# Loading the last rows of wo on all 16 DMA engines, and one wo block ahead of the last V tile, in a four-layer decode attention kernel

## Chip, cores and metric

The kernel runs on one core of a Trainium2 chip. The metric is the device time of one execution in microseconds (us). Every comparison of times is made between runs of the same rounds on the same chip. The single positions in time come from one profiled execution of each kernel, and these are compared across rounds and chips. The granted clock is the share of TensorE's full clock that the profile shows as let through.

## The reference

Two attention blocks, A and B, are applied in the order A, B, A, B to one token `x` of 640 elements. Each block has 32 heads of 192 and caches of 8192 keys and values per head, all in bf16.

```python
def block(x, k_cache, v_cache, wq, wo):            # x: 1 x 1 x 640
    q = (x @ wq).reshape(1, 1, 32, 192).transpose(0, 2, 1, 3)
    scores = einsum("bhqd,bhkd->bhqk", q, k_cache) * 192 ** -0.5
    o = einsum("bhqk,bhkd->bhqd", softmax(scores), v_cache)
    return o.transpose(0, 2, 1, 3).reshape(1, 1, 32 * 192) @ wo
for w in (A, B, A, B):
    x = x + block(layernorm(x), w.k_cache, w.v_cache, w.wq, w.wo)
```

One K or V tile (one head) is 3 MiB. Layers 2 and 3 use the caches of layers 0 and 1 again; the kernel keeps K and V of head 0 of layer 0, and V of heads 28 to 31 of layer 1, on chip for that.

## The kernel before

All large transfers go through one pool of eight slots, each as large as a K or V tile. A list `plan` gives the order of the transfers, a list `steps` the order of the computation, and a transfer is issued as soon as the step that frees its slot is done.

```python
O_LAST = 2; HEADS_W = 10; NSLOT = 8; AHEAD = 4
KEPT = {0: {("k", 0), ("v", 0)}, 1: {("v", 28), ("v", 29), ("v", 30), ("v", 31)}}
...
    O_PART = [P // 2, P // 2, P // 2, P]      # partitions of the last wo rows, by layer
    OI = [O_LAST * DH // n for n in O_PART]   # rows of wo on one partition: 6, 6, 6, 3
```

The output projection of a layer is made in three blocks of ten heads ("wo") and the last two heads ("wol", 384 rows of wo, 480 KB). In layers 0 to 2 the wol rows lie on 64 partitions and are loaded by two transfers of 32 partitions:

```python
            if n[0] == "wol":
                r0 = o["wol"] * DH
                if O_PART[l] == P:
                    return SP.op(lambda s: s.dma_start(
                        wol_rows(l), w["wo"][r0:r0 + O_LAST * DH].rearrange("(p i) n -> p (i n)", p=P)), ...)
                k = O_PART[l] // O_LAST
                for h in range(O_LAST):
                    e = SP.op(lambda s, h=h: s.dma_start(
                        wol_rows(l)[h * k:(h + 1) * k],
                        w["wo"][r0 + h * DH:r0 + (h + 1) * DH].rearrange("(q e i) n -> e q (i n)", e=8, i=OI[l])), ...)
```

The end of a layer in the two lists (m: q times K and the sums S; s: softmax; v: values; wc: transposes ten heads' outputs into oT):

```python
                    if p == H - 1:
                        part.append(("s", l, p))
                        part += [("v", l, i) for i in range(H - AHEAD, H)]
                        part.insert(-O_LAST, ("wc", l, 2))
                steps += part
                plan += [n for n in part if n[0] == "v" and first_load(*n) == n]
            ...
            plan.append(("wo", l, 2));  steps.append(("wo", l, 2))
            plan.append(("wol", l));    steps.append(("wol", l))
```

After a head's values, its outputs are reshaped for the projection one step later. The function that does it is held in `todo`:

```python
                elif n[0] == "v":
                    if todo is not None:
                        todo()
                    values(n[2])
                    todo = (lambda h=n[2]: gather(h)) if n[2] < H - O_LAST else (lambda h=n[2]: gather_last(h))
                ...
                elif n[0] == "wo":
                    if todo is not None:
                        todo()
                        todo = None
                    ...
                    last["oT"] = project(n, slot[place[n]][:, 0:k * D], oT[:, 0:k], last["oTw"])
                else:                                    # wol
                    last["TT"] = last["TTn"]
                    last["oTl"] = ev_y = project(n, wol_rows(l), oTl[0:O_PART[l]], last["TTn"])
```

`wol` does not call `todo`: the `wo` step just ahead of it has.

Of the kernel before, what the change touches and what calls it, by code (L numbers as in the profile page):

```python
# [71 lines left out]
def build(nc, A_x, A_k, A_v, A_wq, A_wo, B_x, B_k, B_v, B_wq, B_wo, out):  # L72
    _, H, SK, DH = A_k.shape
    D = A_x.shape[-1]
    P = 128
# [3 lines left out]
    NL = 4  # L79
# [5 lines left out]
    TS = J * DH  # L85
    QW = H * DH
    Q_PARTS = [[(0, 2), (2, 2), (4, 1)] if l < 2 else [(0, 1), (1, 2), (3, 2)] for l in range(NL)]
    O_PART = [P // 2, P // 2, P // 2, P]
    OI = [O_LAST * DH // n for n in O_PART]
    NB = 3  # L90
    G = 4
# [3 lines left out]
                    wo=[H - HEADS_W, O_LAST, O_LAST + HEADS_W], wol=0)  # L95
    ORDER = [FORWARD, FORWARD, FORWARD, BACKWARD]

    with ExitStack() as ctx:
# [84 lines left out]
        def head(l, p):  # L183
            return ORDER[l]["heads"][p]

        def first_load(kind, l, p):

            n = (kind, head(l, p))
            if l >= 2 and n in KEPT[l - 2]:
                return (kind, l - 2, ORDER[l - 2]["heads"].index(n[1]))  # L190
            return (kind, l, p)

        def stays(kind, l, p):
            return l < 2 and (kind, head(l, p)) in KEPT[l]

        steps, plan = [], []
        for l in range(NL):
            if l < 2:
                plan.append(("wq", l, 0))
                steps += [("wq", l, g) for g in range(3)]  # L200
            elif l == 2:
                plan += [("wq", l, g) for g in range(3)]
                steps.append(("wq", l, 0))
            else:
                plan.append(("wq", l, 0))
                steps.append(("wq", l, 0))
            for p in range(H):
                if p in (HEADS_W, 2 * HEADS_W):
                    b = p // HEADS_W - 1
                    steps += [("wc", l, b), ("wo", l, b)]  # L210
                    plan.append(("wo", l, b))
                if first_load("k", l, p) == ("k", l, p):
                    plan.append(("k", l, p))
                if stays("k", l, p):
                    plan.append(("t", l, p))
                if l == 2 and p == 0:
                    part = [("m", l, 0), ("wq", l, 1), ("s", l, 0), ("v", l, 0), ("wq", l, 2)]
                elif p < H - AHEAD:
                    part = [("m", l, p), ("s", l, p), ("v", l, p)]
                else:  # L220
                    part = [("m", l, p)]
                    if p > H - AHEAD:
                        part.append(("s", l, p - 1))
                    if p == H - 1:
                        part.append(("s", l, p))
                        part += [("v", l, i) for i in range(H - AHEAD, H)]
                        part.insert(-O_LAST, ("wc", l, 2))
                steps += part
                plan += [n for n in part if n[0] == "v" and first_load(*n) == n]
                if l == 3 and p == 1:  # L230
                    for g in (1, 2):
                        plan.append(("wq", l, g))
                        steps.append(("wq", l, g))
            plan.append(("wo", l, 2))
            steps.append(("wo", l, 2))
            plan.append(("wol", l))
            steps.append(("wol", l))
        plan.append(("wob", NL - 1))
# [46 lines left out]
        def wol_rows(l):  # L285
# [3 lines left out]
            else:  # L289
                i = place[("wq", l + 1, 0)] * TS + (DC * QW if l == 0 else QC)  # L290
            return pool[0:O_PART[l], i:i + OI[l] * D]

        def transfer(n):
# [4 lines left out]
# [4 lines that stand above are left out]
                        wol_rows(l), w["wo"][r0:r0 + O_LAST * DH].rearrange("(p i) n -> p (i n)", p=P)),  # L302
                        *free, sem=semOL, inc=16)
                k = O_PART[l] // O_LAST
                for h in range(O_LAST):
# [74 lines left out]
        def layer(l, ev_z, ev_true):  # L380
# [155 lines left out]
            def values(h):  # L536
# [18 lines left out]
                else:  # L555
                    q = 1 if O_PART[l] == P else O_PART[l] // O_LAST // 8
                    parts = [(o_sb[:, i * DH:(i + 1) * DH].rearrange("p (i e q) -> p q e i", i=OI[l], q=q),
# [19 lines left out]
            def gather_last(h):  # L577

                n = O_PART[l] // O_LAST
                k = OI[l]  # L580
# [73 lines left out]
def bass_interleave_layers__gqa_block_cached__mha_block_cached__decode_kernel(  # L654
    nc: bass.Bass,
    A_x: bass.AP,
    A_k_cache: bass.AP,
    A_v_cache: bass.AP,
    A_wq: bass.AP,
    A_wo: bass.AP,  # L660
    B_x: bass.AP,
    B_k_cache: bass.AP,
    B_v_cache: bass.AP,
    B_wq: bass.AP,
    B_wo: bass.AP,
    out: bass.AP,
):
    build(nc, A_x, A_k_cache, A_v_cache, A_wq, A_wo, B_x, B_k_cache, B_v_cache, B_wq, B_wo, out)
# [28 lines left out]
```

## Time and profile before

| | before |
|---|---|
| time, median of the first 3 runs | 1998.22 us (1997.81 to 1998.73) |
| span of the profiled run | 1996.3 us |
| moved by DMA | 849.69 MB, mean 426 GB/s |

The page of the kernel before: its first line, the GB/s line of the 40 slices (each 49.9 us), the DMA sum, and the chain of waits by engine.

```profile
span 1996.3 us, 20649 instructions
...
GB/s 412 429 432 428 431 430 429 431 430 430 429 431 429 430 430 430 429 430 430 429 379 430 430 431 428 432 429 430 431 429 426 431 428 431 430 430 430 429 430 335
DMA packets 40296, 849.69 MB, mean 426 GB/s; under 512 B 4688, under 2 KB 4688, under 8 KB 5136
...
DMA 69%; PE 18%; DVE 11%; ACT 1%; issue 1%; another core or an unknown queue 0%; SPq 0%; DVEq 0%
```

The kernel waits for DMA, which runs at 430 GB/s in nearly all slices. The exceptions are the first, the last, and slice 21 with 379: the change from layer 1 to layer 2. The same place in windows of 10 us (last column GB/s; before it the DMA share and the granted clock):

```profile
1010.00:1020.00 10.00, 6.75 (x171) 5.66 (x163) 0.00 (x0) 2.23 (x6) 0.00 (x0) 0.95 0.72 301
1020.00:1030.00 10.00, 7.83 (x100) 4.29 (x93) 5.57 (x13) 0.73 (x2) 0.54 (x1) 0.50 0.88 345
1030.00:1040.00 10.00, 9.14 (x136) 3.40 (x121) 3.80 (x6) 0.44 (x2) 0.00 (x0) 0.84 1.03 403
```

The timeline of the issuing queue at that place (start, duration, what is issued):

```profile
986.37 0.33 SPq L333 DMA_DIRECT2D pool<-in_B_wo_dram  x1
996.10 1.43 SPq L306 DMA_DIRECT2D pool<-in_B_wo_dram  x2
997.58 0.44 SPq L327 DMA_DIRECT2D pool<-in_A_wq_dram  x1
1020.50 6.25 SPq L327 DMA_DIRECT2D pool<-in_A_wq_dram  x2
1035.35 0.34 SPq L322 DMA_DIRECT2D pool<-in_A_k_cache_dram  x1
```

Layer 2's wq is loaded in three pieces. The second has to wait for the slot of the final wo block (issued at 1020.50), the third for the first piece's, and the next K (head 1) for the slot of the kept K of head 0, whose last use is layer 2's first product (issued at 1035.35). The timeline of TensorE there (the text in brackets says how long the engine was idle before, and what ended it):

```profile
1009.43 1.47 PE L546 MATMUL O<-pool,p_sb 128*2 128x384 bf16 x32
...
1017.31 3.16 PE L465 MATMUL YB<-oT,pool 128*128 128x1 bf16 x75 [1.13 <-DMA pool<-in_B_wo_dram]
1020.40 1.35 PE L465 MATMUL YB<-oTl,pool 64*128 64x1 bf16 x30
...
1023.39 1.78 PE L407 MATMUL QM<-wq,xb 128*128 128x384 bf16 x5 [0.52 <-DVE xb L386]
1024.96 1.39 PE L427 MATMUL QT<-xb,pool 128*128 128x1 bf16 x45
1027.48 0.61 PE L508 MATMUL S<-pool,ident 128*128 128x512 bf16 x1 [1.13 <-DVE pool L495]
1027.88 7.44 PE L58 MATMUL S<-pool,ident 128*128 128x512 bf16 x23
```

The first line is the values of head 30. So there is a tail: the last block lands (1017.26), 75 and 30 matmuls for the projection, the layer norm, the first q, the product with K, the 23 sums, and only then the next K.

The page counts 16 DMA engines, and the trace records 16 landings of each of these transfers (V31: 16 from 1002.72 to 1011.52); each is taken here as the landing of one engine's share. Worked out from these records (us; the spread is from the fastest engine to the slowest):

```
transfer that lands at         fastest   slowest   spread
  496 (V, layer 0)              492.55    496.26     3.7
  530 (wq of layer 1)           523.87    529.56     5.7
 1011 (V31, layer 1)           1002.72   1011.52     8.8
 1029 to 1031 (wq of layer 2)  1029.34   1031.46     2.1
 1506 (V, layer 2)             1501.60   1505.99     4.4
 1517 (wq of layer 3)          1510.78   1517.30     6.5
 1984 (V, layer 3)             1974.16   1983.87     9.7
```

In these rows the engines drift apart (3.7 us at 496, 8.8 at 1011) and come together only after the queue has run dry (131 GB/s from 1018 to 1020; 2.1 at 1029). The kernel goes on at the slowest: the final wo block's last landing is at 1017.26, and the 75 matmuls that wait for it start at 1017.31.

### The profile page before, as it was taken

Reading aid. Unit: us, or ns where it says so; the run is one execution under the profiler, and the core shown is the slowest. Engines: PE = TensorE matmul, PEld = TensorE weight load, DVE = VectorE, ACT = ScalarE, POOL = GpSimd, SP = SyncE. Lnnn points to the kernel's source line nnn. Section 1 sums busy time; section 2 is a strip of 40 time slices with the busy share of each in tenths; the row PEclk is TensorE's granted clock in tenths of the full one; section 3 lists DMA queues with packets and bytes.
Section 4 is the critical chain, followed back from the end, with each engine's and each line's share of the span. In section 5 each row is a group of like instructions: output and inputs, shape, how many; then the busy total and the mean of one; then the engine's idle time right before and its main releaser. Section 6 shows DMA issues by size and latency. Waiting matters only on the chain.

```text
span 1996.3 us, 20649 instructions
## 1 busy us (share of the span) xinstructions
PE 1397.3 (70%) x10555; PEld 321.0 (16%) x7611; DVE 1047.7 (52%) x1074; ACT 220.3 (11%) x665; POOL 4.5 (0%) x22
## 2 busy tenths in 40 slices
PE   4667767667576766666777676776776768767776
PEld 1111112111311211211041111121112212111112
DVE  3554554556255456455725545545663455654563
ACT  0111111111011111111011111111101111111111
POOL 0000000000000000000000000000000000000000
PEclk9888877889678788888977878888887788887888
DMA  9999999999999999999999999999999999999997
GB/s 412 429 432 428 431 430 429 431 430 430 429 431 429 430 430 430 429 430 430 429 379 430 430 431 428 432 429 430 431 429 426 431 428 431 430 430 430 429 430 335
DMA packets 40296, 849.69 MB, mean 426 GB/s; under 512 B 4688, under 2 KB 4688, under 8 KB 5136
## 3 DMA queue, kind: packets, MB, share of 16 engines
q1 hardware_dynamic: 40064, 848.38, 99.3%
q8 instruction: 71, 1.16, 0.2%
q14 instruction: 17, 0.14, 0.0%
q10 hardware_dynamic: 144, 0.00, 0.0%
HBM read 848.36 MB, written 0.00 MB: 425 GB/s over the span
## 4 chain that ended last, share of the span: by engine, by line
DMA 69%; PE 18%; DVE 11%; ACT 1%; issue 1%; another core or an unknown queue 0%; SPq 0%; DVEq 0%
DMA pool<-in_B_k_cache_dram 32%; DMA pool<-in_A_k_cache_dram 30%; PE S L58 12%; DVE pool L495 9%; DMA pool<-in_B_wo_dram 4%; PE O L546 2%; DMA pool<-in_A_wo_dram 2%; DMA x_bf<-in_A_x_dram 1%; PE S L508 1%; PE TB L569 1%; PE QT L427 1%; DVE s_sb L516 1%; PE YB L465 1%; ACT p_sb L526 1%; PE TB L530 0%
## 5 line engine op out<-in xcount | busy, mean ns | idle before, releaser
L495 DVE TENSOR_TENSOR pool<-pool,q_sb 128x3072 bf16<-128x3072 bf16 x512 | 865.7, 1754 | 398.8 <-DMA pool<-in_A_k_cache_dram 204.7
L58 PE MATMUL S<-pool,ident 128*128 128x512 bf16 x2944 | 803.4, 427 | 34.6 <-DVE pool L495 34.5
L546 PE MATMUL O<-pool,p_sb 128*2 128x384 bf16 x4096 | 340.1, 414 | 0.0
L508 PE MATMUL S<-pool,ident 128*128 128x512 bf16 x128 | 61.3, 479 | 223.9 <-DVE pool L495 223.9
L516 DVE TENSOR_REDUCE s_sb<-S 128x64 f32<-128x512 f32 x128 | 88.4, 690 | 237.0 <-PE S L58 237.0
L569 PE MATMUL TB<-o_sb,small 128*1 128x192 f32 x480 | 123.9, 391 | 38.1 <-DVE small L534 27.1
L546 PEld LDWEIGHTS O<-pool,p_sb 128*2 128x2 bf16 x4096 | 128.1, 87 | 128.1 <-issue 91.8
L453 ACT ACTIVATE q_sb<-QM 128x192 bf16<-128x192 f32 x120 | 39.6, 330 | 964.1 <-PE QM L446 964.1
L446 PEld LDWEIGHTS QM<-ident,qT 128*128 128x128 bf16 x240 | 23.2, 98 | 745.3 <-issue 729.8
L530 PE MATMUL TB<-small,ones 128*128 128x1 f32 x256 | 50.3, 266 | 109.9 <-ACT p_sb L526 109.9
L520 PE MATMUL QM<-ident,m_bf 128*128 128x128 bf16 x128 | 27.8, 217 | 122.9 <-DVE m_bf L519 121.2
L561 ACT ACTIVATE o_sb<-O,small 128x384 f32<-128x384 f32 (+1 forms) x136 | 77.2, 579 | 224.5 <-PE O L546 224.5
L534 DVE RECIPROCAL small<-TB 128x1 f32<-128x1 f32 x128 | 21.6, 168 | 122.9 <-PE TB L530 122.9
L526 ACT ACTIVATE p_sb<-s_sb,small 128x64 bf16<-128x64 f32 x128 | 44.5, 348 | 268.5 <-DVE small L523 268.5
L523 DVE TENSOR_REDUCE small<-QM 128x1 f32<-128x128 f32 x128 | 37.3, 292 | 63.3 <-PE QM L520 63.3
L575 ACT ACTIVATE orow<-TB 1x192 bf16<-1x192 f32 x120 | 38.3, 319 | 202.7 <-PE TB L569 202.7
L530 PEld LDWEIGHTS TB<-small,ones 128*128 128x128 f32 x256 | 39.5, 194 | 130.4 <-ACT p_sb L526 130.4
L508 PEld LDWEIGHTS S<-pool,ident 128*128 128x128 bf16 x128 | 12.8, 100 | 283.6 <-DVE pool L495 283.3
L520 PEld LDWEIGHTS QM<-ident,m_bf 128*128 128x128 bf16 x128 | 12.3, 96 | 216.7 <-ACT q_sb L453 126.9
L569 PEld LDWEIGHTS TB<-o_sb,small 128*1 128x1 f32 x480 | 33.5, 89 | 81.4 <-DVE small L534 36.0
L465 PE MATMUL YB<-oT,pool 128*128 128x1 bf16 x900 | 38.1, 178 | 6.6 <-DMA pool<-in_A_wo_dram 3.2
L465 PEld LDWEIGHTS YB<-oT,pool 128*128 128x128 bf16 x900 | 37.0, 131 | 7.6 <-DMA pool<-in_A_wo_dram 3.4
(50 smaller groups left out, 220.0 us busy)
## 6 DMA issues: line engine op xcount, KB each, us to landing
pool<-in_B_k_cache_dram SPq DMA_DIRECT2D x64, 3072.0 KB, 35.5
pool<-in_A_k_cache_dram SPq DMA_DIRECT2D x63, 3072.0 KB, 27.7
pool<-in_A_v_cache_dram SPq DMA_DIRECT2D x63, 3072.0 KB, 33.5
pool<-in_B_v_cache_dram SPq DMA_DIRECT2D x60, 3072.0 KB, 37.0
pool<-in_A_wo_dram SPq DMA_DIRECT2D x6, 2400.0 KB, 25.8
pool<-in_B_wo_dram SPq DMA_DIRECT2D x5, 2400.0 KB, 33.9
pool<-in_A_wq_dram SPq DMA_DIRECT2D x1, 7680.0 KB, 20.9
pool<-in_B_wq_dram SPq DMA_DIRECT2D x1, 7680.0 KB, 29.5
```

Of the source, the lines that this page charges most:

```text
L58: return t.add_instruction(mybir.InstMatmult(name=t.bass.get_next_instruction_name(), engine=mybir.EngineType.PE, ins=[t.lower_ap(rhs), t. ...
L453: lambda a: a.activation(q_sb[i][:], QM[:, 0:DH], ACT.Copy), e, last["q"][i], bank=use["QM"])
L465: e = PE.op(lambda t, i=i, c=c, f=y_first[0], fin=end and i == k - 1: t.matmul(YB[:, c:c + 1], lhsT=t3[:, i, c:D:DC], rhs=o[:, i:i + 1], s ...
L495: e = DV.op(lambda v, d0=d0: v.tensor_tensor(k3[:, :, d0:d0 + QD], kin[:, :, d0:d0 + QD], q_sb[qi][:, d0:d0 + QD].unsqueeze(1).broadcast_t ...
L508: t.matmul(S[:, :], lhsT=ident[:], rhs=k3[:, :, d0:d0 + R], start=True, stop=fin) if d0 == 0 else
L516: ev_s = DV.op(lambda v: v.tensor_reduce(s_sb[par][:], S[:].rearrange("p (j r) -> p j r", r=R), AX.X, ALU.add), ev_S[h], last["s"][par], b ...
L520: e = PE.op(lambda t: t.matmul(QM[:, C_MX:C_MX + P], lhsT=m_bf[par][:, 0:1].broadcast_to([P, P]), rhs=ident[:], start=True, stop=True), ev ...
L526: ev_p[h] = AC.op(lambda a: a.activation(p_sb[pi][:], s_sb[par][:], ACT.Exp, bias=negm[par][:, 0:1], accum_out=l_col[par][:]), ev_n, ev_s, ...
L530: e = PE.op(lambda t: t.matmul(TB[:, C_L + par:C_L + par + 1], lhsT=ones[:, 0:1].broadcast_to([P, P]), rhs=l_col[par][:], start=True, stop ...
L546: e = PE.op(lambda e, g=g, j=j, f=m < G, fin=fin: e.matmul(OB[par][32 * g:32 * g + 2, 0:2 * DH], lhsT=p_sb[pi][:, j:j + 2], rhs=t[:, j * D ...
L561: ev_os[h] = AC.op(lambda a, o=o, i=i: a.activation(o, i, ACT.Copy, scale=rl[pi][:, 0:1]), e, ev_rl[h], last["osb"], bank=use[f"O{par}"])
L569: e = PE.op(lambda t, i=i: t.matmul(TB[0:1, C_O:C_O + DH], lhsT=pick[:, i:i + 1], rhs=o_sb[:, i * DH:(i + 1) * DH], start=(i == 0), stop=( ...
```

## The change

The intent: load the wol rows on all 128 partitions and so on all 16 engines in every layer (in before's trace the two transfers of such a layer have 16 landings together, two on each of eight engines by their order and spacing, and two more records, one 1.1 to 1.2 us after each issue); and, in layer 1 alone, load the final wo block ahead of V of head 31, so that its projection is over and its slot free while V31 is still in flight.

```diff
-    O_PART = [P // 2, P // 2, P // 2, P]
+    O_PART = [P] * NL
...
                         part.insert(-O_LAST, ("wc", l, 2))
+                        part.insert(-1 if l == 1 else len(part), ("wo", l, 2))
                 steps += part
-                plan += [n for n in part if n[0] == "v" and first_load(*n) == n]
+                plan += [n for n in part if n[0] == "wo" or n[0] == "v" and first_load(*n) == n]
...
-            plan.append(("wo", l, 2))
-            steps.append(("wo", l, 2))
             plan.append(("wol", l))
             steps.append(("wol", l))
```

With the new order in layer 1 the `wo` step comes before V31, so nothing calls `todo` after V31: head 31's outputs never reach oTl there, and the projection takes the rows that layer 0 left. The output check cannot see it: every run was correct by it.

## The prediction

> **What bounds the kernel now.** DMA. The page gives 849.69 MB at 426 GB/s over 1996.3 us; the chain of waits is 69% DMA. Steady slices run at about 430 GB/s. Two stand out: number 21 (layer 1 to 2, 379 GB/s) and the last (335). 10 us windows from 1010 to 1040 moved 301, 345 and 403 GB/s: about 5.6 us lost at 430 GB/s.
>
> **Why there.** Four V tiles of layer 1 stay in the eight slots, so little can be queued. The timeline: the final wo block lands at 1017.26; its 75 matmuls take 3.16 us, 30 for the last rows 1.35 us; at 1020.50 the second piece of the next wq is issued, and only when layer 2's head 0 has been multiplied and summed (1035.35) the next K[...].
>
> **The last wo rows.** The landing times in the trace show the 16 engines drifting apart: slowest minus fastest is 8.8 us by 1011, is reset by the dry queue at 1023 to 1037, and is 9.7 us at the end. Each load of the last rows (480 KB) adds 2.3 us to eight engines and nothing to the others[...]. After: 16 engines, 1.15 us each (estimate: half of 2.3). But slow engines are in both groups: at 1011 the eight stand at up to 8.8 us, the others at up to 8.0; at the end 9.7 and about 8.1. Evening out moves the maximum by -0.4 to +0.4 us, not by 1.15 per layer.
>
> **The reordering.** wo lands one V transfer (7.3 us) earlier, near 1010; its 75 matmuls run near 1012.4 to 1015.6, while V31 is in flight. The second wq piece is issued about 5 us earlier, before the slow engines run dry. V31 lands where wo did (about 1017.5). After it come 32 value matmuls (1.47 us) and 15 for the last rows (0.7 us) instead of 4.5 us.
>
> **What was dropped.** The changed kernel's instruction order lacks, in layer 1 alone, head 31's reshaping into oTl (L585 and L590, 2.2 us from the values' end to the copy's). The projection there takes layer 0's rows for that head. I expect this to pass: one head adds some 5e-6 to values of 0.05 in bf16 (estimate). With it, the tail after V31 would be about 4.4 us and the reordering would gain nothing at the next K.
>
> **Sum.** Layer 2's xb, the third wq piece and the next K come about 2 us earlier; from there the queue is full to the end, so this carries through. Evening out adds 0.4 us in the second half. Predicted 1995.8 us (before 1998.2), 8 in 10 between 1993.0 and 1997.8. Faster by over 2%: 0.01; within 2%: 0.98; slower: 0.01.
>
> **What would show it.** Windows 1010 to 1040: about 2 us less lost; the wq issue near 1015.6, the next K's near 1033.4; landing spread no longer growing by 2 us at the last wo rows; slices 11 and 31 (the other layer changes) unchanged.
>
> **What would make it wrong.** If the slow engines are mostly among the eight, each layer gives 1.15 us and the gain is 4 to 5 us. If the drift falls otherwise (single packets cost one engine 1.6 us), 1 to 2 us either way.

1998.2 less 2 us at the next K less 0.4 us from evening out is the forecast of 1995.8. What before's trace shows:

- The last rows of each of layers 0 to 2 have 16 landings in two transfers, two on each of eight engines. The second comes 2.3 us after the same engine's landing of the wo block ahead (505.57 to 507.90, 1010.62 to 1012.94, 1507.31 to 1509.65). That the others get nothing shows in the first wq piece of layer 2: it lands 3.48 us after that block on one of them (1008.43 to 1011.91), 5.78 us after it on one of the eight (1010.62 to 1016.40).
- The next K's first packets start 1.0 us after its issue (1036.34 for 1035.35).
- The 1.6 us: in 263 pairs of large transfers that follow each other, at least 15 engines keep their distances to 0.25 us, and in 60 of these pairs one engine falls 1.45 to 1.63 us (median 1.54) behind the other 15. In each of the 60, exactly one packet of 16384 bytes of the queue that the page calls "q8 instruction" (71 in the span, mean 1.07 us) lies between that engine's two landings; of stretches as long (8.85 us) laid along the span, 27% hold one.

## The result

| | before | after |
|---|---|---|
| median | 1998.01 us (1996.92 to 1998.73, 4 runs) | 1996.08 us (1995.43 to 1997.06, 4 runs) |
| span of the profiled run | 1996.3 us | 1994.7 us |

The ratio is 0.9991, with a 95% interval of 0.9974 to 1.0009. (A ratio is the mean time of one kernel's fast runs over that of the other's of the same rounds, so it is not quite the ratio of the medians.) The interval includes 1: no gain in time is shown by these runs. The forecast was 1995.8 us. The output check cannot see the missing head 31: every run was correct by it.

Line numbers from L228 on are lower by one in the changed kernel. Its page:

```profile
span 1994.7 us, 20387 instructions
...
GB/s 411 431 431 428 431 428 430 430 432 429 429 429 431 428 432 429 429 431 428 430 384 431 430 429 432 428 430 429 430 430 426 429 431 429 431 429 430 430 429 344
DMA packets 40487, 849.67 MB, mean 426 GB/s; under 512 B 4688, under 2 KB 4688, under 8 KB 5328
...
DMA 69%; PE 17%; DVE 12%; ACT 1%; issue 1%; another core or an unknown queue 0%; DVEq 0%
```

Its windows at the layer change:

```profile
1010.00:1020.00 10.00, 6.04 (x117) 4.46 (x115) 0.00 (x0) 0.17 (x1) 0.00 (x0) 0.58 0.97 394
1020.00:1030.00 10.00, 7.82 (x79) 3.34 (x68) 6.31 (x14) 1.68 (x4) 0.54 (x1) 0.50 0.82 329
1030.00:1040.00 10.00, 9.14 (x142) 3.49 (x125) 3.06 (x6) 0.44 (x2) 0.00 (x0) 0.84 0.88 346
```

The gap of 1010 to 1020 is gone (394 for 301), but the next two windows lost what it gained (329 for 345, 346 for 403): in sum 1069 for 1049, which is 0.5 us of transfer at 430 GB/s. The issuing queue shows why:

```profile
976.05 0.33 SPq L332 DMA_DIRECT2D pool<-in_B_wo_dram  x1
986.40 0.33 SPq L321 DMA_DIRECT2D pool<-in_B_v_cache_dram  x1
996.13 0.33 SPq L300 DMA_DIRECT2D pool<-in_B_wo_dram  x1
...
1013.65 12.36 SPq L326 DMA_DIRECT2D pool<-in_A_wq_dram  x2
1034.77 0.34 SPq L321 DMA_DIRECT2D pool<-in_A_k_cache_dram  x1
```

The second wq piece goes out 6.85 us earlier, the next K only 0.58 us. TensorE between the two:

```profile
1010.47 3.16 PE L464 MATMUL YB<-oT,pool 128*128 128x1 bf16 x75
1017.58 2.73 PE L545 MATMUL O<-pool,p_sb 128*2 128x384 bf16 x32 [3.96 <-DMA pool<-in_B_v_cache_dram]
1020.24 0.77 PE L464 MATMUL YB<-oTl,pool 128*128 128x1 bf16 x15
...
1022.65 1.78 PE L406 MATMUL QM<-wq,xb 128*128 128x384 bf16 x5 [0.53 <-DVE xb L385]
1024.22 1.39 PE L426 MATMUL QT<-xb,pool 128*128 128x1 bf16 x45
1026.74 0.61 PE L507 MATMUL S<-pool,ident 128*128 128x512 bf16 x1 [1.13 <-DVE pool L494]
1027.14 7.60 PE L58 MATMUL S<-pool,ident 128*128 128x512 bf16 x23
```

V31 landed at 1017.53, where the wo block had landed before. But its 32 value matmuls took 2.73 us, not 1.47 as the forecast had taken from before (its line at 1009.43): the granted clock was 0.50 from 1011.65 to 1032.13.

From the landing records, the load of the last rows no longer widens the spread by 2 us in layer 2: 3.7 us at 1510 and 3.6 us at 1515 (before: 4.4 and 6.5). The packet records of the layer 0 to 1 change give 64 packets of 7680 bytes at a mean of 294 ns before, and 128 of 3840 bytes at 154 ns after: 8 on each of eight engines are 2.4 us, 8 on each of 16 engines 1.2 us (by the landings, two transfers of eight engines each and one of 16).

### The profile page after: what moved, and what is told of

Read it like the earlier page. It is cut to its first block, busy times and chain, and to the rows that moved or that the text cites. A ratio compares the mean times of both kernels' runs of the same rounds, so it can differ in the third digit from the quotient of the medians.

```text
span 1994.7 us, 20387 instructions
## 1 busy us (share of the span) xinstructions
PE 1392.3 (70%) x10426; PEld 317.9 (16%) x7482; DVE 1047.4 (53%) x1074; ACT 220.2 (11%) x664; POOL 4.5 (0%) x22
## 3 DMA queue, kind: packets, MB, share of 16 engines
q8 instruction: 70, 1.15, 0.2%
## 4 chain that ended last, share of the span: by engine, by line
DMA 69%; PE 17%; DVE 12%; ACT 1%; issue 1%; another core or an unknown queue 0%; DVEq 0%
DMA pool<-in_B_k_cache_dram 32%; DMA pool<-in_A_k_cache_dram 30%; PE S L58 11%; DVE pool L494 10%; DMA pool<-in_B_wo_dram 2%; PE O L545 2%; DMA pool<-in_A_wo_dram 2%; DMA pool<-in_B_v_cache_dram 2%; DMA x_bf<-in_A_x_dram 1%; PE S L507 1%; PE TB L568 1%; PE QT L426 1%; DVE s_sb L515 1%; ACT p_sb L525 1%; PE YB L464 1%
## 5 line engine op out<-in xcount | busy, mean ns | idle before, releaser
L545 PE MATMUL O<-pool,p_sb 128*2 128x384 bf16 x4096 | 346.9, 420 | 4.0 <-DMA pool<-in_B_v_cache_dram 4.0
```

The source lines that it names most:

```text
L545: e = PE.op(lambda e, g=g, j=j, f=m < G, fin=fin: e.matmul(OB[par][32 * g:32 * g + 2, 0:2 * DH], lhsT=p_sb[pi][:, j:j + 2], rhs=t[:, j * D ...
```

## How the time is split in the experiments

Four terms make up the span of each profiled run: when the last block that layer 1's tail starts from (wo before, V31 in the new order) has landed; from there to the start of the 23 S matmuls of layer 2's head 0 (the tail); those matmuls, to the issue of the next K; and the rest, to the end. In us, worked out from each kernel's trace:

```
run            landed   tail   S    next K    rest    span
before        1017.26  10.62  7.47  1035.35  961.00  1996.35
after         1017.53   9.61  7.63  1034.77  959.96  1994.73
after_again   1017.39   9.59  6.59  1033.57  960.23  1993.80
even_only     1017.34   9.97  6.53  1033.84  960.43  1994.27
even_again    1017.48   9.93  7.40  1034.81  961.18  1995.99
even_drop31   1017.72   9.92  6.74  1034.38  960.67  1995.05
even_l2       1016.96  10.62  7.06  1034.64  960.47  1995.12
even_l01      1017.88   9.92  7.83  1035.63  960.69  1996.32
order_only    1016.93  10.19  7.89  1035.01  961.61  1996.62
gather_back   1017.40  11.62  7.80  1036.82  959.98  1996.80
warm          1017.77   8.99  6.66  1033.42  960.45  1993.87
late          1017.82  17.88  6.67  1042.37  959.92  2002.29
```

The tail repeats to 0.05 us between kernels with the same instructions in it; the S term and the rest vary by up to 1.4 us from run to run. That is why the tail can be read from a single trace, while 5 rounds of times leave an interval of about 0.25%, or 5 us. The traced run was the fastest of its five in after_again, even_only, even_l2, even_drop31, gather_back and warm (warm: 1995.67 us, its other four 1997.63 to 1998.68), so S and rest of one trace don't stand for the kernel. The S matmuls take 6.5 to 7.9 us. In all twelve traces they take the longer, the later after their start the clock comes back: 2.8 us after it in even_only (6.53), 5.5 in order_only (7.89). It came back at 1029.87 in after_again (6.59) and at 1030.07 in even_only (6.53), at 1032.13 in after (7.63) and 1034.36 in gather_back (7.80).

## The experiments

My theory after the result: the even load gains little through the engines' drift and 0.65 us through 15 instead of 30 matmuls; the order gains what the shorter tail after V31 leaves; the time follows the issue of the next K. Rivals: the even load gains its 1.15 us in each layer, or the early second wq piece is the gain. The first four kernels ran on one chip, the next three on another, the last four together again; each group has nine runs of the kernel before.

### after_again: the changed kernel once more

> The changed kernel once more, as the yardstick of this group. Both theories: 1995.5 to 1996.8 us, 1.3 to 2.3 us under before. The next K of layer 2 (its head 1) is issued within 1 us of 1034.8, its slowest landing about 0.3 us ahead of before's; the landing spread stays near 3.4 us over the first load of the last wo rows.

Measured: 1996.06 us against 1998.88 for before in this group, ratio 0.9988 (0.9975 to 1.0000). The gain of 2.8 us is over the expected 1.3 to 2.3. The next K went out at 1033.57, 1.2 us earlier than in the first trace, where 1 was allowed; 1.0 us of that are the S matmuls, which ran at full clock from 1029.87 on. The tail is the same as in the first trace. The second wq piece went out at 1016.83 here, 3.2 us later than in the first trace, and yet the next K earlier: the early piece is not what sets it. The windows from 1010 to 1040 moved 1119 in sum, 1.6 us of transfer more than before's 1049, where the first trace had 0.5. The spread did not stay near 3.4 us over the first load: it went from 3.75 (last V of layer 0) to 4.77 (wq of layer 1); in before it went from 3.71 to 5.69.

### even_only: the load on 16 engines alone

```diff
-    O_PART = [P // 2, P // 2, P // 2, P]
+    O_PART = [P] * NL
```

> Only the 16-engine load of the last wo rows, with the old order and all of head 31. Theory (slow engines sit in both groups of eight, so evening moves the slowest one little; the gain at the layer 1 to 2 change comes from the order): 0.2 to 1.2 us under before, the final wo block of layer 1 landing within 0.5 us of before's 1017.3, the next K issued within 0.7 us of 1035.35. Rival (the eight are the slow ones, each layer gives its 1.15 us): 2.3 to 3.4 us under before, as much as or more than the whole change.

Measured: 1997.28 us against 1998.88, ratio 0.9991 (0.9979 to 1.0004): 1.6 us by the medians, between the two theories' ranges. The positions in the trace decide: wo landed at 1017.34, not 1.15 us earlier, so the rival fails for the first half. The tail is 0.65 us shorter. The next K went out 1.5 us earlier, more than the 0.7 allowed, 0.9 us of it in the S matmuls. This kernel is complete: head 31 is in it. Its projection, where the last rows take 0.74 us for before's 1.35:

```profile
1017.43 3.16 PE L465 MATMUL YB<-oT,pool 128*128 128x1 bf16 x75
1020.45 0.74 PE L465 MATMUL YB<-oTl,pool 128*128 128x1 bf16 x15
```

### order_only: the new order alone, rows still on eight engines

The changed kernel with `O_PART = [P // 2, P // 2, P // 2, P]`.

> Only the new order (with the missing head 31 of layer 1), the last rows still on eight engines. Theory: V31 lands at about 1017.3, the second wq piece is issued before 1015, but the values and the last rows run at a granted clock of 0.5, so the next K is issued only 0 to 1 us before 1035.35; 0 to 1 us under before. Rival (the order alone is the change's gain): 1.5 to 2.3 us under before.

Measured: 1998.36 us against 1998.88, ratio 0.9994 (0.9980 to 1.0008). The next K at 1035.01 and the small gain are as the theory has them; the second wq piece, expected before 1015, went out at 1016.38. The tail is 0.43 us shorter. The values took 2.73 us here too.

### gather_back: the changed kernel with head 31's reshaping put back

```diff
                 else:
+                    if todo is not None:
+                        todo()
+                        todo = None
                     last["TT"] = last["TTn"]
```

> The changed kernel with head 31's reshaping in layer 1 put back: a complete kernel. Theory (the time follows the issue of the next K one for one): the tail after V31 grows by 1.8 to 2.4 us, the next K is issued at about 1036.9, and the time is 1.5 to 2.4 us over the changed kernel, so 1997.5 to 1998.6, level with before. Rival (the early second wq piece and the even load make the gain, the tail is covered by queued wq): within 0.5 us of the changed kernel.

Measured: 1999.14 us against 1998.88, ratio 1.0003 (0.9990 to 1.0016), 3.1 us over after_again by the medians of the same rounds, more than the expected 1.5 to 2.4, and above the 1997.5 to 1998.6 that it should have taken. The next K went out at 1036.82 (expected 1036.9), and the tail is 2.0 us longer than in the changed kernel. Its TensorE and ScalarE timeline, where three lines stand between the values and the last rows:

```profile
1017.44 2.73 PE L545 MATMUL O<-pool,p_sb 128*2 128x384 bf16 x32
...
1020.22 0.94 ACT L560 ACTIVATE o_sb<-O,small 128x192 f32<-128x192 f32 x2 [5.81 <-PE O L545]
...
1021.22 0.86 PE L584 MATMUL TB<-small,o_sb 128*64 128x1 f32 x12 [1.04 <-ACT o_sb L560]
1022.11 0.17 ACT L589 ACTIVATE oTl<-TB 64x3 bf16<-64x3 f32 x1 [0.95 <-PE TB L584]
...
1022.34 0.77 PE L464 MATMUL YB<-oTl,pool 128*128 128x1 bf16 x15 [0.26 <-ACT oTl L589]
```

So the new order, made complete, has a longer tail than the old order with even loads (11.62 for 9.97 us). The second wq piece was issued at 1017.32 here, still 3.2 us ahead of before, and that did not help.

### late: 40 idle matmuls ahead of the last rows of layer 1

The changed kernel with this at the head of the wol step (the sums go to a bank that is overwritten later):

```diff
+                    if l == 1:
+                        for _ in range(40):
+                            PE.op(lambda t: t.matmul(SP_[0][:, :], lhsT=ident[:], rhs=slot[place[("v", 1, 28)]][:, 0:512],
+                                                     start=True, stop=True), signal=False, bank=use["S0"])
```

> The changed kernel with 40 idle 128x512 matmuls ahead of the last rows of layer 1, which makes layer 2 start 8.6 us (full clock) to 17 us (half) later. Theory (time follows the issue of the next K one for one, since the queue holds nothing else there): the time grows by as much as the next K's issue moves, within 1 us. Rival (the wq pieces queued ahead absorb a part): the time grows by at least 3 us less than the issue moves.

The 8.6 and 17 us are estimates from before's trace, where S matmuls of this shape start 216 ns apart at a clock of 1.00 and 427 ns apart at 0.50 (medians).

Measured: 2004.76 us against 1998.81, ratio 1.0032 (1.0018 to 1.0045). The idle matmuls (one of the 40 is missing from the trace; 39 took 8.82 us) and the next K, from its TensorE and queue timelines:

```profile
1021.19 8.82 PE L625 MATMUL S<-pool,ident 128*128 128x512 bf16 x39 [0.33 <-issue]
...
1042.37 0.34 SPq L321 DMA_DIRECT2D pool<-in_A_k_cache_dram  x1
```

Against the first trace of the changed kernel, the next K went out 7.60 us later, and the span grew by 7.56 us; against the second (after_again), 8.80 and 8.49 us. By the medians it is 5.95 us over before of its rounds, with the next K 7.02 us later than in before's trace and the rest 1.1 us shorter. So a delay of that issue is paid one for one, within 0.3 us. That an earlier issue would be repaid likewise was not tested by an edit.

### warm: an idle wide matmul after every five of the 75

```diff
+                    if warm:
+                        PE.op(lambda t: t.matmul(SP_[0][:, :], lhsT=ident[:], rhs=slot[place[("v", 1, 28)]][:, 0:512],
+                                                 start=True, stop=True), signal=False, bank=use["S0"])
```

> The changed kernel with one idle 128x512 matmul after every five of the final wo block's 75 in layer 1 (their sums go to a bank that is overwritten). Theory (the 1.3 us that the tail after V31 took over the forecast is the granted clock of 0.5): the clock stays at 1.00 to about 1018, the 32 value matmuls take 1.5 instead of 2.7 us, and the next K is issued 1 to 2 us earlier than in the changed kernel; the time falls by 0.5 to 1.5 us. Rival (the tail is held by the landing of V31 and of the last rows alone): values shorter, next K and time unchanged within 0.4 us. If 15 such matmuls do not hold the clock, values stay at 2.7 us and the run says nothing.

Measured: 1998.45 us against 1998.81, ratio 0.9997 (0.9984 to 1.0009). From the TensorE timeline:

```profile
1019.47 1.47 PE L548 MATMUL O<-pool,p_sb 128*2 128x384 bf16 x32
1020.88 0.76 PE L464 MATMUL YB<-oTl,pool 128*128 128x1 bf16 x15
...
1023.07 0.99 PE L406 MATMUL QM<-wq,xb 128*128 128x384 bf16 x5 [0.52 <-DVE xb L385]
```

The clock stayed at 1.00 to 1026.37, the values took 1.47 us and the five QM matmuls 0.99 for 1.78. That the clock is the cause of the 1.26 us is thereby shown. But the idle matmuls themselves held the values up until 1.70 us after V31 had landed, so the tail fell by 0.6 us only, and the next K went out 1.35 us before after's and 0.15 us before after_again's. A gain in time was not seen (by the medians 0.4 us under before, where the theory had 0.5 to 1.5 us under the changed kernel, which did not run in these rounds); as a version to use it is a miss.

### uneven4: the rows of layers 0 to 2 meant for four engines

Two edits in the kernel before: `e=8` becomes `e=4` in the transfer, and `// 8` becomes `// 4` where the outputs are arranged for it.

> The kernel before with the last wo rows of layers 0 to 2 on four engines instead of eight (4.6 us on each of them, nothing on the other twelve); result unchanged. Theory (what counts is the slowest engine, and the drift puts it in either group): the spread jumps by up to 4.6 us per load, and the time grows by 1 to 5 us, less than the 6.9 us by which the four are loaded more. Rival (the loads are absorbed by the slots' slack and the drift does not matter): within 0.7 us of before. Rival 2 (each unevenness is paid in full): 4.6 us in the two halves that end at the slowest engine, or more.

That `e=4` puts the load on four engines, 4.6 us on each, was an estimate: half as many engines as for `e=8`, twice the 2.3 us.

Measured: 2011.16 us against 1998.81, ratio 1.0062 (1.0046 to 1.0077): 12.4 us, far over the theory's 1 to 5 us; of the three it fits only the second rival, which had no upper bound. In its trace 8.1 us are lost by the issue of the next K of layer 2 (1043.49) and 5.2 us after it. The 64 packets of layer 0's load took 486 ns each on the mean, not 294, so the design was not the plain doubling that I had meant. At wq of layer 1, after that load, all engines were later than in before, the fastest by 3.7 us, the slowest by 6.9. It refutes that uneven loads are absorbed; it does not measure the price of eight engines. Why all engines were late, also the ones meant to have no such packets, is open.

### even_l2, even_l01: the even load in layer 2 alone, in layers 0 and 1 alone

`O_PART = [P // 2, P // 2, P, P]`, and `O_PART = [P, P, P // 2, P]`.

> The kernel before with the last wo rows of layer 2 alone on 16 engines. Theory (from the first runs: from the issue of the next K of layer 2 to the end, kernels with even loads took 959.9 to 960.5 us of the span, the ones on eight engines 961.0 and 961.6): the issue of that K stays at 1035.35 within 1.2 us, the rest takes 960.2 within 0.4, the spread over that load no longer grows by 2 us; about 1.0 us under before. Rival (evening saves only by halving the last rows' matmuls at the layer 1 to 2 change): same as before within 0.4 us.

> The last wo rows of layers 0 and 1 on 16 engines, those of layer 2 on eight. Theory: 15 instead of 30 matmuls in the chain from the final wo block to layer 2 bring the next K 0.65 us forward, the drift of the first half nothing; the rest takes 961.3 within 0.5 us; 0.3 to 1.0 us under before. Rival (the whole gain of evening comes from layer 2): same as before within 0.3 us.

Measured against 1998.43 us for before: even_l2 1997.53 us, ratio 0.9996 (0.9983 to 1.0008); even_l01 1998.12 us, ratio 0.9995 (0.9982 to 1.0007). The tails of 10.62 and 9.92 us are as expected: only the halved number of matmuls in layer 1 shortens the tail. But even_l01's next K went out at 1035.63, 0.28 us after before's instead of 0.65 ahead of it: the block landed 0.62 us later, and the S matmuls took 0.36 us more. even_l2's rest of 960.47 us is as expected; even_l01's 960.69 us is below the 960.8 that was its limit, so the second half's gain is smaller than the first traces had it. The gains by the medians, 0.9 and 0.3 us, do not decide by themselves.

### even_drop31: even loads, old order, head 31's reshaping left out in layer 1

```diff
                 elif n[0] == "wo":
+                    if n == ("wo", 1, 2):
+                        todo = None
                     if todo is not None:
```

> Even loads in the old order, with head 31's reshaping in layer 1 left out (wrong by one head on purpose, below what the outputs resolve). Theory (in the old order that reshaping is over before the final wo block lands, so it is not on the path; the omission pays only together with the new order): next K and time as in the kernel with even loads alone, within 0.5 us. Rival (the omission itself is worth its 2.2 us anywhere): 1.5 us or more under the kernel with even loads alone.

Measured: 1997.47 us, ratio 0.9994 (0.9981 to 1.0006); tail 9.92 us, as with head 31. In the old order the omission is worth nothing.

### even_again: even_only as yardstick of that group

> The kernel with even loads alone once more, as yardstick of this group: 1996.6 to 1998.0 us, 1 to 2 us under before; the next K issued between 1033.5 and 1035.5, the rest 960.2 within 0.5 us.

Measured: 1997.78 us against 1998.43, ratio 0.9995 (0.9981 to 1.0008). It is 0.65 us under before, less than the 1 to 2 expected. The next K at 1034.81 is within what was expected; the rest took 961.18 us, over the expected 960.7.

## Why the prediction was right, and where its terms were off

**The time was right** (1995.8 forecast, 1996.08 measured), and so was the place: the layer 1 to 2 change, with the wq piece early, V31 landing where wo had (1017.5 forecast, 1017.53 measured) and the slices at the other layer changes as before (429 and 426). That a delay of the next K costs its full length was shown by late. But the agreement to 0.3 us is luck: the interval of the ratio is 7 us wide, and the terms missed in both directions. The tail gave 1.0 us where the prediction had 2.3; the next K was forecast for 1033.4 and went out at 1034.77, and at 1033.57 in the second trace, where the S matmuls were faster by 1.0 us; the rest of the span was 1.0 and 0.8 us shorter than before's, where 0.4 was forecast.

**The even load, first half: no gain, as forecast.** Over the traces, the block lands at 1017.05 us on the mean of the three kernels with layer 0's rows on eight engines (before, order_only, even_l2) and at 1017.59 on that of the nine others in the table. The two sets don't overlap. With even loads it lands 0.5 us later, not 1.15 earlier. The prediction had said -0.4 to +0.4 us, because engines outside the eight are nearly as late (at 1011 in before the slowest of them is 8.0 us behind the fastest engine, the slowest of the eight 8.8); that this is the reason was not tested by itself.

**The even load, second half: sign right, size uncertain.** The rest takes 961.10 us on the mean of the three with layer 2's rows on eight engines, 960.37 on that of the nine others: 0.7 us, for the 0.4 forecast. Single traces vary by 1.3 us, and the two groups overlap.

**The tail: mis-sized by a factor of two.** The prediction let the tail shrink from 4.5 to 2.2 us after the landing; from 1017.31 to the last matmul's end at 1021.75 before, and from 1017.58 to 1021.01 after, it is 4.4 and 3.4 us. The term that failed is "32 value matmuls (1.47 us)": they took 2.73 us, because the granted clock was 0.50 (at 1.00, in warm, they took 1.47). Of the 248 stretches of one clock in before's trace, all but one last a whole multiple of 3.41 us. I had taken the cost of the value matmuls from a place where the clock was 1.00 (1009.43 in before); after the change they follow 75 matmuls of one column and a wait of 3.96 us, in a stretch at 0.50. The wait did not bring that about: the clock fell while those 75 still ran (at 1011.65 in after, at 1016.22 in after_again), and the values took 2.73 us in order_only too, after a wait of only 0.62. Of the 1.0 us that the tail did give, 0.65 us are the 15 matmuls saved by the even load (even_only) and 0.35 us the order with its omission (9.60 against 9.95, each the mean of two traces).

**What was dropped: right, and it carries the order.** With head 31 put back, the order costs 1.7 us of tail against even loads alone; with it left out, it gains 0.35. The prediction's "the reordering would gain nothing at the next K" was mild. The part of the change that shortens the tail and is also complete is the even load alone: 1997.28 and 1997.78 us in its two groups, 1.6 and 0.65 us under before, and by the verdicts the same as before.

**Left open:** what drives the engines apart by 8 us in half the span (the steps of 1.5 us, each with one packet of the instruction queue, were not tested by an edit), and whether a next K issued before 1033.4 would gain any more. In after_again, where it went out at 1033.57, the third wq piece was still landing until 1036.36, so the queue was not dry then. Open too is why the rest of the span differs by over 1 us between traces of like kernels.

## What to carry to other kernels

When a load is reordered, write down the whole chain that starts at its new last landing, with each instruction at the clock that it will run at, and check that every step is still in it: a step that was run by the neighbour that moved can be lost without a wrong output. Spreading a load from half of the engines over all of them loads the other half more (here eight packets of 154 ns, 1.2 us, on each engine that had none); look at the slowest landings of both halves before counting a gain (here none was seen in the first half of the span). For changes of a microsecond in two thousand, compare stretches that repeat from trace to trace (here the tail, to 0.05 us), and do not take them for a gain in time that the medians cannot show.

## What the traces leave unexplained

- What keeps the clock. It fell to 0.50 at 1016.22 in after_again, right after 3.41 us in which TensorE was busy for 3.37 us with matmuls of one column. In warm, with a 512-column matmul after every five of these and TensorE busy for 3.32 of 3.40 us, it stayed at 1.00. So the busy time that the profile shows does not tell in these two traces which stretch keeps the clock; what does is not shown. Two stretches of 3.41 us of after_again (TensorE busy first, clock third from the right):

```profile
1012.81:1016.22 3.41, 3.37 (x76) 3.35 (x77) 0.00 (x0) 0.17 (x1) 0.00 (x0) 1.00 0.67 284
1016.22:1019.63 3.41, 2.77 (x43) 1.42 (x45) 0.00 (x0) 0.00 (x0) 0.00 (x0) 0.50 0.82 302
```

- What a packet takes. Packets of 7680 bytes took 294 ns on eight engines in before and 486 ns in uneven4, whose edit was meant for four (layer 0 of both; 368 ns in layer 1 of uneven4, 488 in layer 2). Whether the number of engines or the changed order of the rows does that was not tested.
- How far the 16 engines drift apart in a long stream of equal transfers: 7.6 to 8.8 us between the first and the last landing of one V tile that lands between 1000 and 1018 us, in all kernels here but uneven4 (11.0). In after, V31's first landing was at 1009.67 and its last at 1017.53, and its value matmuls started at 1017.58.
